# Bucketed attention and a feed-forward block on one core: the row maxima of heads 1 to 3 at new places, and four smaller moves around them

## The chip, the cores and the metric

The program runs on one core of a Trainium2 chip. The metric is the device time of one execution in microseconds (us). The core has five engines that each work through a queue of their own in order: TensorE (PE, matmuls), VectorE (DVE), ScalarE (ACT), GpSimd (POOL) and SyncE (SP), which here issues the transfers (DMAs). An instruction at the head of a queue that waits for another engine holds up everything behind it on its own engine.

## The reference

```python
q_bits = (einsum('bhsd,dk->bhsk', q, proj) > 0)      # 6 bits a row; k_bits likewise
mask   = q_bucket[..., :, None] == k_bucket[..., None, :]
scores = where(mask, q @ k.T / sqrt(64), -1e9)
attn   = exp(scores - scores.max(-1)); attn = attn / (attn.sum(-1) + 1e-9)
x      = attn @ v                                    # batch 4, 8 heads, 768 rows, width 64
h      = x_as_rows(3072, 512) @ w_in                 # 512 -> 2048
g      = where(h >= 1, h, where(h <= -1, 0, (h + 1)**2 / 4))
out    = g @ w_out                                   # 2048 -> 512
```

All of it is float32. The kernel keeps the accuracy by splitting each operand into a rounded high part and the rest, a low part, and multiplying the parts separately.

## The kernel before, in words

The 32 heads are taken in 16 pairs. A head has 12 **units**, 384 in all, numbered g from 0; head hd has the units from 12·hd. Six units cover one half of the 768 query rows, one for each block of 128 keys. The loop at the end of `attention` (L614) writes the instructions in this order for each unit:

1. `s_unit(g)`: two score matmuls (L372, L373) into one of four PSUM tiles `s`, and two exponentials on ACT (L381, L386).
2. A reduction that the unit before left over.
3. `lo_unit(g-1)`: the low part of the exponentials of the unit before, on DVE, or on POOL for the units with g mod 6 of 0 or 3.
4. `pv_unit(g-4)`: three matmuls with V (L405, L407, L409); the last of six is followed by a copy on ACT (L415) and the transfers of the result.
5. The **tasks** of the unit: whatever `at(g, ...)` put there, in the order in which the calls were made.

**Row maxima.** The mask works through extra rows of the operands: rows 0 to 7 hold the bits of both sides' buckets, and one row of the query side holds a clamped maximum of the masked scores, so that it is subtracted within the matmul. A head's maxima need six pairs of matmuls (`max_mm`, L311) into a PSUM tile `smax`, of which there is one, and six reductions on DVE (`max_red`, L315). The table `early` says where each pair goes, counted in **slots**: slot 5·g+k is in unit g, before the V matmuls (k=2), between them (k=3, 4) or behind them (k=5). For k of 2 to 4 the reduction is written at once, so on DVE it stands behind `lo_unit(g-1)`. For k=5 it is left over to the next unit, where it is written ahead of `lo_unit(g)`; the tasks of unit g stand in front of it.

**From the maxima to the query row.** Head 0 and head 1: `row_clamp` on DVE, three small matmuls on PE and a copy on ACT (`row_half`, L267) into row 32 of tile `T2[0]`. Head 2: `half_clamp` on DVE, `half_put` (a transposition on PE, a copy on ACT, two DMAs) for each half. From head 3 on: `max_clamp` on POOL (L343, L345), `max_tr` (transposition on PE, L350), `max_put` (copy on ACT, L355; two DMAs, L357 and L358). The first DMA writes row 7 of `T2`, which the second score matmul (L373) of the head reads.

**Preparing a pair.** `load_raw` brings q and k of a pair into the one tile `raw`; four times `cast_h` and `low_h` on POOL make high and low parts (L153 and L39 `t<-raw,t`), for head 0 and 1 of the pair and for the first and second half (n = 0 to 3); four `move` DMAs (L164) copy parts to other rows. `bits_mm` (four matmuls, L211), `bits_cmp` (DVE, L222), `bits_scale` (L272 or L274) and `bits_put` (four DMAs) make the bits. `load_v`, `cast_v` (ACT, L290) and `split_v` (POOL) prepare V. Pair p lives in tile p mod 3, so pair 3 takes over the tiles of pair 0, and row 32 of `T2[0]` must be cleared before that (L570).

After the attention, from about 460 us on, come the feed-forward matmuls (L829, L966, L1061). The change touches only the tasks and slots of the first 36 units, which the profile shows between 12 and 64 us.

Of the kernel before, what the change touches and what calls it, by code (L numbers as in the profile page):

```python
# [11 lines left out]
F32 = mybir.dt.float32  # L12
# [13 lines left out]
NJ = S // P  # L26
# [84 lines left out]
NU = 2 * NJ  # L111
SHIFT = 4


def attention(ctx, tc, wst, T1, T2, qk, v, pj, cv, x_d, s_d, e_d, tasks, shared):
    nc = tc.nc
# [340 lines left out]
    def at(g, fn, *a):  # L457
        tasks[g].append((fn, a))
# [79 lines left out]
    for n, g in enumerate((1, 4, 5, 6)):  # L538
        at(g, quarter, n)
    at(6, lambda: nc.gpsimd.memset(T2[1][0:64, 0].bitcast(F32), 0.0))  # L540
    at(7, row_clamp, 1, 0, NJ // 2)
    for n in (0, 1):
        at(8, move, 1, n)
    at(8, bits_mm, 1, 0, 1)
    at(9, bits_cmp, 1, 0)
    at(9, ones_row, 1, nc.vector)
    at(9, row_half, 1, 0)
    at(9, row_flags, 0)
    at(10, bits_mm, 1, 1, 0)
    at(10, split_v, 0, nc.gpsimd, 1)  # L550
# [16 lines left out]
    at(19, half_put, 2, 0, 1)  # L567
    at(23, half_clamp, 2, 1)
    at(25, half_put, 2, 1, 0)
    at(2 * NU + 1, lambda: nc.gpsimd.memset(T2[0][32:33, 0].bitcast(F32), 0.0))  # L570
    for hd in range(NH):
        pr, h = hd // 2, hd % 2
        g = hd * NU
        if 0 < hd < NH - 2:
            gc, gt = ((30, 33), (41, 43))[hd - 1] if hd < 3 else (g + NU + SHIFT - 1, g + NU + SHIFT + 1)
            at(gc, max_clamp, hd + 2, nc.gpsimd)
            at(gt, max_tr, hd + 2)
            at(gt, max_put, hd + 2)
        if h == 0 and pr + 2 < NPAIR:
            g0 = g + (13, 2)[pr] if pr < 2 else g  # L580
            for n in range(4):
                at(g0 + n, cast_h, pr + 2, nc.gpsimd, n % 2, n // 2)
                at(g0 + n, low_h, pr + 2, nc.gpsimd, n % 2, n // 2)
            at(g0 + 3, move, pr + 2, 0)
            at(g0 + 3, move, pr + 2, 1)
            at(g0 + 6, move, pr + 2, 2)
            if pr + 3 < NPAIR:
                at(g0 + 7, load_raw, pr + 3)
            bits_at = ((20, 1), (23, 0)) if pr == 0 else ((8 if pr == 1 else 7, 1), (11, 0))
            for hf, (n, bank) in enumerate(bits_at):  # L590
                at(g + n, bits_mm, pr + 2, hf, bank)
                at(g + n + 1, bits_cmp, pr + 2, hf)
            at(g + n + 1, move, pr + 2, 3)
            at(g + n + (2 if pr else 1), bits_scale, pr + 2, nc.gpsimd if pr else nc.scalar)
            at(g + (18 if pr else 25), bits_put, pr + 2)
        if h == 0 and pr + 1 < NPAIR:
            gv = g + LAG + (2 if pr else 16)
            at(gv, cast_v, pr + 1, nc.scalar)
            at(gv + 1, split_v, pr + 1, nc.gpsimd, 0)
            at(gv + 3, split_v, pr + 1, nc.gpsimd, 1)  # L600
            if pr + 2 < NPAIR:
                at(gv + (6 if pr else 4), load_v, pr + 2)
# [1 line left out]
    NG = NH * NU  # L604
    red = None
    early = {}
    for hd, gs in ((0, (0, 2)), (1, (4, 5, 6, 8, 11, 12)), (2, (15, 16, 17, 19, 20, 22)), (3, (21, 23, 24, 26, 27, 29))):
        early.update({5 * n + 5: (hd, NJ - len(gs) + i) for i, n in enumerate(gs)})
    for i in range(2 * NJ):
        n = 5 * 31 + 35 * i // 4  # L610
        early[n + (n % 5 == 1)] = 4 + i // NJ, i % NJ
# [494 lines left out]
def lsh_attn_ffn(ctx: ExitStack, tc: tile.TileContext, qk, v, pj, cv, w_in, w_out, out):  # L1106
# [101 lines left out]
    for i in (2, 3):  # L1208
        at(NH * NU + 2 * i - 10, late[i + NFT - NW1][0])
    attention(actx, tc, wst, T1, T2, qk, v, pj, cv, x_d, s_d, e_d, tasks, attn)  # L1210
    actx.close()

# [78 lines left out]
```

## Time and profile before

| | |
|---|---|
| median of 3 runs | 979.32 us (979.09 to 982.97) |
| the profiled execution | 979.4 us, of which the span is 977.6 us |
| PE busy | 961.9 us |
| DVE, ACT, POOL busy | 788.3, 680.2, 354.8 us |
| granted PE clock | 1.00 |

A row of the timeline gives the start and the duration in us, the engine, the line of the kernel, the operation, what it writes and reads, shapes, a count, and in brackets the idle time of the engine before it with what ended it. Matmuls overlap: one of 384 columns is shown with some 0.34 us, and the next starts 0.17 to 0.18 us later. SPq rows are issues of DMAs, not the transfers themselves.

### The profile page before, as it was taken

The page shows a single profiled execution, that of the slowest core. Times are in us where ns is not written, and L with a number is a line of the kernel's source. Part 1 is how long each engine was busy: PE and PEld are TensorE (multiplying, and loading weights), DVE is VectorE, ACT ScalarE, POOL GpSimd, SP SyncE. Part 2 cuts the span into 40 slices and gives each one's busy share as a digit, 9 for nine tenths or more (in the row PEclk, how much of TensorE's full clock was granted, in tenths as well). Part 3 has the DMA queues.
Part 4 walks back from the last instruction along what each step waited for, and adds up shares of the span by engine and source line. Part 5 has one row for each costly group of instructions (what it writes and reads, how often), then busy time and mean ns, then how long its engine had stood idle before and what let it go on. Part 6 is the DMA issues. An engine that isn't in the chain of part 4 may idle for free.

```text
span 977.6 us, 15547 instructions
## 1 busy us (share of the span) xinstructions
PE 961.9 (98%) x5050; PEld 890.3 (91%) x5050; DVE 788.3 (81%) x1355; ACT 680.2 (70%) x1481; POOL 354.8 (36%) x422
## 2 busy tenths in 40 slices
PE   8999999999999999999999999999999999999998
PEld 7889999999999999999999998888988888888896
DVE  8779999999999999897898788787776777655554
ACT  7888998989989998987755565455564545544444
POOL 8768887777788877566000000000000000000000
PEclk9999999999999999999999999999999999999999
DMA  5775566677666666635494479976459554454431
GB/s 161 191 183 157 153 170 177 175 191 197 179 167 166 157 175 176 153 114 134 128 335 162 139 227 300 295 241 201 119 160 236 146 183 118 148 154 119 119 87 65
DMA packets 95113, 167.56 MB, mean 171 GB/s; under 512 B 13956, under 2 KB 51960, under 8 KB 95032
## 3 DMA queue, kind: packets, MB, share of 16 engines
q1 hardware_dynamic: 94808, 166.56, 60.7%
q8 instruction: 40, 0.66, 0.3%
q14 instruction: 41, 0.34, 0.1%
q10 hardware_dynamic: 224, 0.00, 0.0%
HBM read 106.13 MB, written 33.87 MB: 143 GB/s over the span
## 4 chain that ended last, share of the span: by engine, by line
PE 86%; DVE 5%; POOL 5%; ACT 1%; issue 1%; DMA 1%; DVEq 0%; POOLq 0%; ACTq 0%
PE y L829 27%; PE h L1061 18%; PE h L966 7%; PE smax L311 6%; PE s L373 5%; PE s L372 5%; PE o L405 5%; PE o L407 5%; PE o L409 5%; POOL t L39 3%; PE o L211 2%; DVE nm L315 2%; DVE pl L39 1%; POOL pl L39 1%; POOL t L153 1%
## 5 line engine op out<-in xcount | busy, mean ns | idle before, releaser
L381 ACT ACTIVATE ph<-s 128x384 fp32r<-128x384 f32 x380 | 188.6, 496 | 41.2 <-PE s L373 36.1
L315 DVE TENSOR_REDUCE nm<-smax 128x1 f32<-128x768 f32 x189 | 179.3, 949 | 22.2 <-PE smax L311 21.0
L39 POOL TENSOR_TENSOR pl<-pf,ph 128x384 fp32r<-128x384 f32 x128 | 134.1, 1052 | 78.8 <-ACT pf L386 78.8
L794 DVE SCALAR_TENSOR_TENSOR t<-t 128x384 f32<-128x384 f32 x128 | 71.2, 557 | 101.0 <-ACT z L789 100.8
L39 DVE TENSOR_TENSOR pl<-s,ph 128x384 fp32r<-128x384 f32 x256 | 135.4, 545 | 10.9 <-ACT s L386 9.0
L372 PE MATMUL s<-t 128*128 128x384 f32 x384 | 132.2, 344 | 0.0
L373 PE MATMUL s<-t 128*128 128x384 f32 x384 | 129.6, 337 | 1.7 <-DMA t<-te 1.7
L409 PE MATMUL o<-pl,va 128*128 128x386 f32 x384 | 130.4, 340 | 0.4 <-DVE pl L39 0.4
L407 PE MATMUL o<-ph,vb 128*128 128x386 f32 x384 | 130.0, 339 | 0.0
L405 PE MATMUL o<-ph,va 128*128 128x386 f32 x384 | 129.9, 338 | 0.0
L386 ACT ACTIVATE s<-s 128x384 f32<-128x384 f32 x252 | 125.5, 498 | 0.0
L829 PE MATMUL y<-t,ghi 128*128 128x512 f32 x384 | 124.7, 395 | 0.0
L311 PE MATMUL smax<-t 128*128 128x384 f32 x378 | 100.1, 346 | 4.5 <-DVE nm L315 4.4
L788 ACT ACTIVATE t<-h,mh 128x384 f32<-128x384 f32 x56 | 32.5, 581 | 82.2 <-PE h L966 43.5
L799 ACT CAST ghi<-z 128x384 fp32r<-128x384 f32 x129 | 65.1, 505 | 30.6 <-DVE z L795 26.9
L789 ACT ACTIVATE z<-t,m 128x384 f32<-128x384 f32 x128 | 79.0, 617 | 4.2
L829 PEld LDWEIGHTS y<-t,ghi 128*128 128x128 f32 x384 | 71.3, 188 | 11.1 <-ACT ghi L799 0.3
L1061 PE MATMUL h<-wbig,t 128*128 128x384 f32 x399 | 81.4, 336 | 0.0
L311 PEld LDWEIGHTS smax<-t 128*128 128x128 f32 x378 | 66.6, 188 | 14.5 <-DVE nm L315 13.7
L1061 PEld LDWEIGHTS h<-wbig,t 128*128 128x128 f32 x399 | 71.6, 188 | 5.2
L788 ACT ACTIVATE t<-wsq,mh 128x384 f32<-128x384 f32 x48 | 29.6, 617 | 66.7 <-DVE wsq L1074 40.4
L829 PE MATMUL y<-t,glo 128*128 128x512 f32 x192 | 76.0, 396 | 0.0
(190 smaller groups left out, 2142.9 us busy)
## 6 DMA issues: line engine op xcount, KB each, us to landing
t<-wc SPq DMA_DIRECT2D x92, 256.0 KB
t<-t SPq DMA_DIRECT2D x60, 384.0 KB
wraw<-wc SPq DMA_DIRECT2D x76, 256.0 KB
raw<-in_qk_dram SPq DMA_DIRECT2D x14, 768.0 KB
wraw<-in_w_in_dram SPq DMA_DIRECT2D x16, 512.0 KB
wraw<-in_w_out_dram SPq DMA_DIRECT2D x16, 512.0 KB
t<-ed SPq DMA_DIRECT2D x36, 192.0 KB
xd<-xs SPq DMA_DIRECT2D x32, 192.5 KB
```

Source lines behind the costliest of these rows:

```text
L39: eng.tensor_tensor(out=out, in0=a, in1=b, op=ALU.subtract)
L311: nc.tensor.matmul(out=smax[hd][:, hf, 0:HS], lhsT=t2[:, 0, h, i * P:(i + 1) * P], rhs=t2[:, 1, h, hf * HS:(hf + 1) * HS], start=True, sto ...
L315: nc.vector.tensor_reduce(out=nmp(hd)[:, i:i + 1], in_=smax[hd][:, :, 0:HS], axis=AX.XY, op=ALU.max, negate=True)
L372: nc.tensor.matmul(out=ps[:, 0:HS], lhsT=t1[:, 1, h, ks], rhs=t1[:, 0, h, sl], start=True, stop=False)
L373: nc.tensor.matmul(out=ps[:, 0:HS], lhsT=t2[:, 1, h, ks], rhs=t2[:, 0, h, sl], start=False, stop=True)
L381: nc.scalar.activation(out=ph[:, 0:HS], in_=ps[:, 0:HS], func=AF.Exp, scale=SCALE)
L386: nc.scalar.activation(out=pf, in_=ps[:, 0:HS], func=AF.Exp, scale=SCALE)
L405: nc.tensor.matmul(out=o, lhsT=wa, rhs=ph, start=(jj == 0), stop=False)
L407: nc.tensor.matmul(out=o, lhsT=wb, rhs=ph, start=False, stop=False)
L409: nc.tensor.matmul(out=o, lhsT=wa, rhs=pl, start=False, stop=(jj == NJ - 1))
L829: nc.tensor.matmul(out=ys[c][m], lhsT=g_[:, m * P:(m + 1) * P], rhs=w, start=(first and k == 0), stop=(last and k == 2))
L1061: nc.tensor.matmul(out=ps, lhsT=w[:, cs], rhs=x, start=(n == 0 and s not in (2, 3, 6)), stop=(n == 5), skip_group_check=True)
```

## The change

- **Slots.** Heads 1, 2 and 3 had their maxima at k=5 of units 4, 5, 6, 8, 11, 12; 15, 16, 17, 19, 20, 22; and 21, 23, 24, 26, 27, 29. Now they stand at slots 25, 32, 40, 47, 57, 65; 72 to 109; and 117 to 150, some 7.4 slots apart, at k of 2, 4 and 5. Heads 0, 4 and later keep theirs.
- **Head 1.** The first `row_clamp` and `row_half` stand one unit later (8 and 10).
- **Pair 3** (the fourth pair). Of its four cast-and-low steps, which stood in units 26 to 29, the first two stay and the others go to 31 and 32. Its moves 0 and 1 go from unit 29 to 32, move 2 from 32 to 35, and the load of the next `raw` from 33 to 36.
- **Head 3.** `max_clamp` stays in unit 30; `max_tr` and `max_put` go from 33 to 31.
- **Row 32** is cleared by two memsets of one head each, in units 20 and 25, in place of one for both in unit 25.

```diff
-    at(7, row_clamp, 1, 0, NJ // 2)
+    at(8, row_clamp, 1, 0, NJ // 2)
...
-    at(9, row_half, 1, 0)
+    at(10, row_half, 1, 0)
...
-    at(2 * NU + 1, lambda: nc.gpsimd.memset(T2[0][32:33, 0].bitcast(F32), 0.0))
+    for h, g in enumerate((20, 2 * NU + 1)):
+        at(g, lambda h=h: nc.gpsimd.memset(T2[0][32:33, 0, h].bitcast(F32), 0.0))
...
-            gc, gt = ((30, 33), (41, 43))[hd - 1] if hd < 3 else (g + NU + SHIFT - 1, g + NU + SHIFT + 1)
+            gc, gt = ((30, 31), (41, 43))[hd - 1] if hd < 3 else (g + NU + SHIFT - 1, g + NU + SHIFT + 1)
...
-            g0 = g + (13, 2)[pr] if pr < 2 else g
+            g0 = g + (13, 5)[pr] if pr < 2 else g
             for n in range(4):
-                at(g0 + n, cast_h, pr + 2, nc.gpsimd, n % 2, n // 2)
-                at(g0 + n, low_h, pr + 2, nc.gpsimd, n % 2, n // 2)
+                gq = g0 + n - (3 if pr == 1 and n < 2 else 0)
+                at(gq, cast_h, pr + 2, nc.gpsimd, n % 2, n // 2)
+                at(gq, low_h, pr + 2, nc.gpsimd, n % 2, n // 2)
...
-    for hd, gs in ((0, (0, 2)), (1, (4, 5, 6, 8, 11, 12)), (2, (15, 16, 17, 19, 20, 22)), (3, (21, 23, 24, 26, 27, 29))):
-        early.update({5 * n + 5: (hd, NJ - len(gs) + i) for i, n in enumerate(gs)})
+    for hd, gs in ((0, (5, 15)), (1, (25, 32, 40, 47, 57, 65)), (2, (72, 79, 87, 94, 102, 109)),
+                   (3, (117, 124, 130, 137, 144, 150))):
+        early.update({n: (hd, NJ - len(gs) + i) for i, n in enumerate(gs)})
```

## The prediction

> **What bounds the kernel now.** I read the page first, then the waits of PE, then the timelines of all engines between 12 and 64 us, where the changed units run.
>
> ```profile
> span 977.6 us, 15547 instructions
> PE 961.9 (98%) x5050; PEld 890.3 (91%) x5050; DVE 788.3 (81%) x1355; ACT 680.2 (70%) x1481; POOL 354.8 (36%) x422
> ```
>
> PE is idle for 977.6 − 961.9 = 15.7 us of the whole span, so no change of order alone can be worth more. The waits of PE between 16 and 62 us, where all the moved maxima lie, and a row from the whole run:
>
> ```profile
> PE smax L311 <- DVE nm L315: 2.0, 8, 0.5
> PE o L261 <- DVE nrow L252: 0.4, 1, 0.4
> ...
> PE s L373 <- DMA t<-te: 1.7, 1, 1.7
> ```
>
> So there are two prizes: 2.0 us over eight waits of maxima for the one `smax` tile, and 1.7 us at one score matmul. Where that one comes from, on PE, on POOL and in the issues of SP:
>
> ```profile
> 54.77 0.62 PE L311 MATMUL smax<-t 128*128 128x384 f32 x2 [0.17 <-DVE nm L315]
> ...
> 58.90 0.27 PE L350 MATMUL s<-ident,nm 128*12 128x128 f32 x1
> ...
> 61.82 0.33 PE L372 MATMUL s<-t 128*128 128x384 f32 x1
> 63.85 0.44 PE L373 MATMUL s<-t 128*128 128x384 f32 x1 [1.70 <-DMA t<-te]
> ```
>
> ```profile
> 50.37 0.50 POOL L153 CAST t<-raw 128x384 fp32r<-128x384 f32 x1 [0.29 <-DMA raw<-in_qk_dram]
> ...
> 53.46 1.01 POOL L39 TENSOR_TENSOR pl<-pf,ph 128x384 fp32r<-128x384 f32 x1
> 54.42 0.50 POOL L153 CAST t<-raw 128x384 fp32r<-128x384 f32 x1
> 55.00 1.02 POOL L39 TENSOR_TENSOR t<-raw,t 128x384 fp32r<-128x384 f32 x1
> ...
> 57.53 0.23 POOL L343 TENSOR_SCALAR nm<-nm 128x6 f32<-128x6 f32 x1
> 57.84 0.23 POOL L345 TENSOR_SCALAR nm<-nm 128x6 f32<-128x6 f32 x1
> ```
>
> ```profile
> 56.49 2.42 SPq L164 DMA_DIRECT2D t<-t  x3
> 60.12 0.76 SPq L357 DMA_DIRECT2D t<-te  x1
> ```
>
> Head 3 begins with unit 36 at 61.82 and needs its row 7. The clamp came at 57.53, behind four casts, the transposition at 58.90, and the DMA was issued at 60.12, behind three moves of 384 KB issued from 56.49 on. It released PE at 63.85, 1.85 us later than the next matmul would have begun (61.82 + 0.18).
>
> **The change, part by part.**
>
> *The transposition two units sooner.* In the changed order head 3's DMA is issued ahead of the moves (units 31 and 32), and two casts stand behind the clamp instead of in front. If the clamp is in time, the 1.85 us go. The clamp can start when POOL has done two casts and the low part of unit 27, at 54.42, and when the last of head 3's reductions has ended. That end is the crux.
>
> *The spacing.* How fast can maxima follow one another through one `smax`?
>
> ```profile
> 33.92 0.62 PE L311 MATMUL smax<-t 128*128 128x384 f32 x2 [0.24 <-DVE nm L315]
> ...
> 35.59 0.62 PE L311 MATMUL smax<-t 128*128 128x384 f32 x2 [0.16 <-DVE nm L315]
> ```
>
> One per 1.67 us, if DVE is free. A spacing of 7.4 slots is 7.4 × 0.175 + 0.35 = 1.65 us of PE's work: level with that, with no slack. What matters then is where the reduction stands on DVE. At k=2 to 4 it is behind the low part of the unit before, which waits for ACT; at k=5 it was ahead of the next one. So I walk through the stretch where ACT is late. These rows of ACT, DVE and PE fix it:
>
> ```profile
> 41.88 0.83 ACT L290 CAST va<-vraw 128x768 fp32r<-128x768 f32 x1 [0.58 <-DMA vraw<-in_v_dram]
> ...
> 44.24 0.53 ACT L386 ACTIVATE s<-s 128x384 f32<-128x384 f32 x1
> ...
> 47.65 1.03 ACT L272 ACTIVATE bits<-neg,cvt 32x768 fp32r<-32x768 f32 x1
> ...
> 50.31 0.46 ACT L381 ACTIVATE ph<-s 128x384 fp32r<-128x384 f32 x1
> ```
>
> ```profile
> 42.13 0.96 DVE L315 TENSOR_REDUCE nm<-smax 128x1 f32<-128x768 f32 x1
> 43.80 0.96 DVE L315 TENSOR_REDUCE nm<-smax 128x1 f32<-128x768 f32 x1 [0.71 <-PE smax L311]
> 44.87 0.56 DVE L39 TENSOR_TENSOR pl<-s,ph 128x384 fp32r<-128x384 f32 x1
> 45.34 0.42 DVE L326 TENSOR_SCALAR nmh<-nm 128x3 f32<-128x3 f32 x1
> ...
> 45.75 0.94 DVE L315 TENSOR_REDUCE nm<-smax 128x1 f32<-128x768 f32 x1
> 46.61 0.54 DVE L39 TENSOR_TENSOR pl<-s,ph 128x384 fp32r<-128x384 f32 x1
> 47.08 0.54 DVE L222 TENSOR_TENSOR neg<-o,neg 32x384 f32<-32x384 f32 x1
> ...
> 53.76 0.96 DVE L315 TENSOR_REDUCE nm<-smax 128x1 f32<-128x768 f32 x1 [0.22 <-PE smax L311]
> ```
>
> ACT waited for V of pair 1 until 41.88. That load was issued behind the bits of pair 1 and two moves. Their start hangs on the comparison of unit 11, and in the new order one more reduction (slot 57) stands in front of that. What PE wins in units 5 to 10, some 0.6 us, is lost there, so I leave 41.88 where it is. Then unit 22's exponential ends at 44.24 + 0.53 = 44.77 as before. From there, by the new order on DVE:
>
> - low part of unit 22 at 44.8; behind it the reduction of slot 117, at 44.8 + 0.47 = 45.27, ending at 46.2. Before, head 3's first reduction had run at 42.13, inside ACT's delay.
> - slot 124 on PE at 46.3. Its reduction starts behind `half_clamp` and the low part of unit 23 (46.1 + 0.5 + 0.47), at 47.1, and takes a step of 0.87.
> - the comparison of pair 2's bits, which now stands behind that reduction: 48.0 to 48.5, against 47.08 to 47.62.
> - so ACT's bits at 48.55 instead of 47.65: 0.9 us later. ACT took from 47.65 to the row at 50.31, the first of unit 27, to finish unit 26; by that, 2.7 us, unit 26 is finished at 51.2 to 51.3, and its low part runs at 51.3.
> - the reduction of slot 137 stands behind this low part: 51.3 + 0.47 = 51.8. Slots 144 and 150 then go at the rate of the single tile, 1.67 us each: the last reduction of head 3 starts at 55.1 and ends at 56.1, against 53.76 + 0.96 = 54.72.
> - slot 155, head 4's first, waits for that and starts at 56.1, against 54.77: PE is 1.35 us **later** here than before.
>
> From there to unit 36 PE does the same work as before, 61.82 − 54.77 = 7.05 us, so unit 36 begins at 63.2 and its second matmul at 63.35. Head 3's DMA no longer stops it: clamp from 56.1 to 56.7, transposition about 57.4 (56.1 + 0.35 + a unit of 0.88), issue at some 58.5, which by the 63.85 − 60.12 = 3.7 us of the old one, moves in front of it and all, lands at 62.2.
>
> The sum: −1.85 for the wait and +1.35 for the later last reduction, −0.5 us in all.
>
> *The smaller parts.* These rows price them, the last two of SP.
>
> ```profile
> 25.25 0.47 ACT L267 CAST t<-smax 1x384 fp32r<-1x384 f32 x1
> ...
> 42.79 1.01 POOL L39 TENSOR_TENSOR vb<-vraw,va 128x384 fp32r<-128x384 f32 x1 [3.69 <-ACT va L290]
> ...
> 48.70 1.38 POOL L570 MEMSET t<- 1x1536 f32 x1
> ```
>
> ```profile
> 43.62 0.59 SPq L148 DMA_DIRECT2D raw<-in_qk_dram  x1
> ...
> 62.40 0.38 SPq L148 DMA_DIRECT2D raw<-in_qk_dram  x1
> ```
>
> Head 1's first half of the query row is copied a unit later, some 26.3 instead of 25.72 with unit 12 at about 27: hidden by one unit's matmuls, and at most the 0.47 of the copy if PE gets there early. The memset of 1.38 becomes two of about 0.69 (half the elements; between 0.2 for launch alone, as a clamp row shows, and 1.38). The first falls into POOL's idle 3.69 us before 42.79. The second saves nothing, because the casts behind it wait for `raw` at 50.37. So 0, from both sides. The three moves and the next `raw` are only issued later: nothing but head 3's two DMAs stands in between on SP, and pair 4's first cast, below, runs at 76.36, 14 us after the old issue (62.40), against 6.75 for the earlier load of that size (issued at 43.62, used at 50.37). 0 here too; at worst the three units of delay, some 3.9 us at 1.3 a unit (54.77 to 61.82 is five and a half), which that margin covers.
>
> **The rivals.**
>
> *A, the whole prize.* If DVE is not held up as I walk it, for instance because V lands sooner, the last reduction stays at 54.72 or before. Then the clamp is bound by POOL alone, 54.42 + 0.5 = 54.9, and PE passes the transposition at about 55.0, where unit 32 began at 56.09 before: 1.05 us sooner, and 1.85 more at unit 36, together 2.9. Time 979.4 − 2.9 = 976.5. For it speaks that PE's work there leaves room. Against it, the single tile at 1.67 per maximum.
>
> ```profile
> 56.09 0.33 PE L372 MATMUL s<-t 128*128 128x384 f32 x1
> ```
>
> *B, slower: POOL becomes the bound at unit 35.* The two casts behind the clamp are needed by the second `bits_mm` of pair 3 there. In my walk POOL goes from the clamp's end, 56.7, through four subtractions at 0.96 (unit 30's low part, one split of V, two low halves of the pair; 53.46 to 54.42 is such a step) and two casts at 0.58 (54.42 to 55.00): 56.7 + 4 × 0.96 + 2 × 0.58 = 61.7. PE comes to it at 63.2 − 0.7 = 62.5, 0.8 us of slack. Later in the run POOL's rows are longer:
>
> ```profile
> L39 POOL TENSOR_TENSOR t<-raw,t 128x384 fp32r<-128x384 f32 x12 | 12.1, 1016 | 0.8
> ...
> 76.36 0.96 POOL L153 CAST t<-raw 128x384 fp32r<-128x384 f32 x1
> ...
> 79.91 1.35 POOL L39 TENSOR_TENSOR t<-raw,t 128x384 fp32r<-128x384 f32 x1
> ```
>
> At 1.35 and 0.96 the same queue takes 4 × 0.34 + 2 × 0.46 = 2.3 more, 1.5 over the slack, and the sum is −0.5 + 1.5 = +1.0: 980.4. It decides from 0.8 us of stretching on; over 1.3 us the kernel is slower. Against it: the twelve subtractions between 12 and 70 us took 1016 ns on average. [...]
>
> *C, it does not do what it says.* The maxima wait as much as before, in other places, and head 3's row is late again, since the clamp follows a last reduction about 2.8 us later than before (57.5): no gain, 979.4.
>
> **How the numbers follow.** My sum is against the profiled execution, 979.4, which stands 0.1 over the median of 979.32. The forecast is 979.4 − 0.5 = 978.9, with a range of its own of 978.0 to 979.8. Chances: forecast 0.5, A 0.27, B 0.13, C 0.1. The range that takes in A and B is 976.2 to 980.8. A measurement of this kernel can tell about 0.5%, 4.9 us, from no change. All my cases lie within that. The bound for more is the sum of all waits of PE in this stretch, 2.0 + 1.7 + 0.4 = 4.1 us with 0.1 to restart after each of ten, 5.1. So faster 0.03, same 0.95, slower 0.02, the rest for causes that I don't see.
>
> **What would show it.** Right: no wait of L373 for `te`; the bits of pair 2 on ACT at 48 to 49; a wait of over 1 us of a maximum for DVE near 51 to 53; PE's waits of L311 for L315 in this stretch well over 2.0 us; slot 155 past 55.5. A is right if the bits stay at 47.65 or earlier and unit 36 begins before 61.5. B shows as a wait of L211 for POOL near 62. The sum is wrong if V lands at another time than 41.9, since the whole walk hangs on it.

## The result, and the profile after

The changed kernel takes 984.33 us in the median of 15 executions (981.82 to 989.01), the kernel before 980.22 (978.86 to 983.4). The ratio is 1.0039, 95% interval 1.0029 to 1.0050: slower by 0.4%, where 0.05% less was forecast. The profiled execution is 7.0 us longer in its span. Page and PE clock by slices:

```profile
span 984.6 us, 15537 instructions
PE 965.2 (98%) x5050; PEld 894.5 (91%) x5050; DVE 787.5 (80%) x1355; ACT 680.0 (69%) x1481; POOL 355.2 (36%) x423
...
PEclk9899999999999999999999999999999999999999
```

The second slice, 25 to 49 us, has a clock below 9 tenths. By stretches (length, then busy time with counts of PE, weight loads, DVE, ACT, POOL; then the granted clock):

```profile
24.00:36.00 12.00, 8.58 (x44) 7.66 (x44) 7.15 (x14) 7.02 (x17) 9.90 (x14) 0.85 0.49 132
36.00:48.00 12.00, 10.71 (x52) 9.97 (x51) 7.56 (x12) 8.61 (x22) 5.82 (x8) 0.86 0.71 176
...
72.00:100.00 28.00, 26.26 (x140) 25.44 (x139) 22.98 (x35) 22.76 (x55) 19.03 (x22) 0.94 0.65 169
```

At a clock of either 1.0 or 0.5, the only two values in the trace's record of it, a mean of 0.85 is 3.6 us at half of it (12 × 0.15 / 0.5), 0.86 is 3.4, 0.94 in 28 us is 3.4: 10.4 us at half clock. (The record itself has 0.5 from 32.51 to 39.34 us and from 83.71 to 87.12, 10.24 us.) The kernel before had 1.00 in all such stretches:

```profile
24.00:36.00 12.00, 11.31 (x63) 9.53 (x62) 8.59 (x14) 10.79 (x25) 11.00 (x15) 1.00 0.53 135
36.00:48.00 12.00, 11.58 (x64) 10.33 (x62) 10.34 (x19) 8.96 (x21) 6.34 (x8) 1.00 0.88 236
```

The waits of PE in the changed kernel between 12 and 100 us (total, times, longest):

```profile
PE smax L311 <- DMA t<-bits: 2.7, 1, 2.7
PE s L373 <- DMA t<-te: 1.7, 1, 1.7
PE o L405 <- DVE neg L222: 1.7, 2, 1.0
PE smax L311 <- DVE nm L315: 1.6, 3, 1.1
PE o L334 <- ACT s L386: 0.5, 1, 0.5
```

The total of waits for reductions has fallen to 1.6 us, from 2.8 in the kernel before over the same stretch, and two waits for transfers head the list. PE's timeline at both places, and at unit 36:

```profile
30.07 0.34 PE L372 MATMUL s<-t 128*128 128x384 f32 x1
30.25 0.33 PE L373 MATMUL s<-t 128*128 128x384 f32 x1
33.27 0.98 PE L311 MATMUL smax<-t 128*128 128x384 f32 x2 [2.69 <-DMA t<-bits]
34.04 0.53 PE L405 MATMUL o<-ph,va 128*128 128x386 f32 x1
34.36 0.53 PE L407 MATMUL o<-ph,vb 128*128 128x386 f32 x1
...
59.79 0.34 PE L372 MATMUL s<-t 128*128 128x384 f32 x1
...
68.06 0.34 PE L372 MATMUL s<-t 128*128 128x384 f32 x1
68.23 0.33 PE L373 MATMUL s<-t 128*128 128x384 f32 x1
...
81.15 0.34 PE L372 MATMUL s<-t 128*128 128x384 f32 x1
83.23 0.44 PE L373 MATMUL s<-t 128*128 128x384 f32 x1 [1.74 <-DMA t<-te]
...
84.30 0.53 PE L407 MATMUL o<-ph,vb 128*128 128x386 f32 x1
```

Unit 14 begins at 30.07, as before (30.08). Slot 72, head 2's first maximum, then waits 2.69 us for pair 1's bits, and the matmuls behind it take 0.53 instead of 0.34 and start 0.32 apart instead of 0.175. Unit 36 goes through without the old stop. At 81.15 unit 48, head 4's first, stops for its row in the way unit 36 used to, and slow matmuls follow again. Head 2's first maximum in the kernel before, at slot 80, for comparison:

```profile
32.22 0.59 PE L311 MATMUL smax<-t 128*128 128x384 f32 x2
```

The first score matmul of a unit shows where each kernel stands. The table gives how many us later than in the kernel before it starts, in the profiled executions. The ratio compares the medians with executions of the kernel before from the same measurement; medians of different rows can come from different measurements. "full" counts the timed executions with a mean granted clock of 0.999 or more.

| kernel | unit 12 | 16 | 30 | 37 | 60 | median, us | ratio to before, 95% | full |
|---|---|---|---|---|---|---|---|---|
| changed | +0.54 | +5.03 | +6.24 | +4.27 | +7.06 | 984.33 | 1.0029 to 1.0050 | 3 of 15 |
| e6 slot 72 alone | −0.11 | +1.32 | +0.57 | +0.58 | +0.57 | 980.43 | 1.0002 to 1.0020 | 9 of 11 |
| e1 slots alone | +4.00 | +7.09 | +8.27 | +6.55 | +6.55 | 982.73 | 1.0023 to 1.0042 | 3 of 12 |
| e2 pair 3 alone | +0.15 | −0.07 | −0.31 | −2.25 | −1.30 | 979.40 | 0.9984 to 1.0010 | 7 of 12 |
| e3 slots 80, 83 | +0.14 | +0.66 | +2.95 | +0.99 | +3.01 | 983.83 | 1.0022 to 1.0051 | 2 of 5 |
| e5 fillers | +0.23 | +2.72 | +3.16 | +1.20 | +2.26 | 982.96 | 1.0014 to 1.0039 | 8 of 12 |
| e7 e3, bits 44 | +0.73 | +1.23 | +3.49 | +1.54 | +2.02 | 981.88 | 0.9999 to 1.0019 | 9 of 11 |
| e8 e2, bits 44 | +0.24 | +0.06 | −0.17 | −2.09 | −1.97 | 978.58 | 0.9964 to 0.9989 | 11 of 12 |
| e9 e3, head 3 old | +0.34 | +0.84 | +1.65 | −0.30 | +0.89 | 982.23 | 1.0001 to 1.0025 | 3 of 11 |
| e10 e9, slots 50, 60 | +1.61 | +1.26 | +2.08 | +0.14 | +1.06 | 981.19 | 0.9994 to 1.0024 | 6 of 12 |
| e11 e1, other clamp | +0.28 | +2.77 | +3.19 | +2.86 | +2.85 | 982.25 | 1.0004 to 1.0024 | 4 of 12 |
| e12 e8, other clamp | −0.37 | −0.37 | −0.59 | −2.19 | −1.97 | 978.08 | 0.9960 to 0.9980 | 11 of 11 |
| e13 e10, other clamp | +0.74 | +0.38 | +1.20 | −0.75 | +0.41 | 981.43 | 0.9991 to 1.0013 | 5 of 12 |

From unit 60 to unit 380 most of them keep their distance to within half a microsecond; e5, e7 and e9 lose another 0.9 to 1.3. Of the kernel before, 20 of 29 executions beside e1 were full, with a median of 979.26; the other nine had 981.48. Of the changed kernel the three full ones had 982.13 and the twelve others 985.47. So, as far as two measurements compare, about 2.9 us of the loss are there at full clock; the rest of the median's 4.1 goes with the clock.

### The profile page after: what moved, and what is told of

It reads as the page before. It is cut to its first block, busy times and chain, and to the rows that moved or that the text cites. A ratio compares the mean times of both kernels' runs of the same rounds, so it can differ in the third digit from the quotient of the medians.

```text
span 984.6 us, 15537 instructions
## 1 busy us (share of the span) xinstructions
PE 965.2 (98%) x5050; PEld 894.5 (91%) x5050; DVE 787.5 (80%) x1355; ACT 680.0 (69%) x1481; POOL 355.2 (36%) x423
## 4 chain that ended last, share of the span: by engine, by line
PE 87%; POOL 5%; DVE 4%; ACT 1%; issue 1%; DMA 1%; SPq 0%; DVEq 0%; POOLq 0%
PE y L832 27%; PE h L1064 18%; PE h L969 7%; PE smax L311 6%; PE s L373 5%; PE s L372 5%; PE o L405 5%; PE o L407 5%; PE o L409 5%; POOL t L39 3%; PE o L211 2%; DVE nm L315 1%; POOL pl L39 1%; DVE pl L39 1%; POOL t L153 1%
## 5 line engine op out<-in xcount | busy, mean ns | idle before, releaser
L315 DVE TENSOR_REDUCE nm<-smax 128x1 f32<-128x768 f32 x189 | 179.3, 949 | 27.7 <-PE smax L311 26.7
L311 PE MATMUL smax<-t 128*128 128x384 f32 x378 | 100.4, 347 | 6.2 <-DVE nm L315 3.1
L311 PEld LDWEIGHTS smax<-t 128*128 128x128 f32 x378 | 67.5, 190 | 14.5 <-DVE nm L315 10.8
L832 PE MATMUL y<-woh,glo 128*128 128x512 f32 x192 | 75.7, 394 | 0.2
```

Source lines behind the costliest of these rows:

```text
L311: nc.tensor.matmul(out=smax[hd][:, hf, 0:HS], lhsT=t2[:, 0, h, i * P:(i + 1) * P], rhs=t2[:, 1, h, hf * HS:(hf + 1) * HS], start=True, sto ...
L315: nc.vector.tensor_reduce(out=nmp(hd)[:, i:i + 1], in_=smax[hd][:, :, 0:HS], axis=AX.XY, op=ALU.max, negate=True)
L832: nc.tensor.matmul(out=ys[c][m], lhsT=g_[:, m * P:(m + 1) * P], rhs=w, start=(first and k == 0), stop=(last and k == 2))
```

## The experiments

The theory formed after the result, W, is that PE stops for transfers that the change calls for too early (pair 1's bits) or issues too late (head 4's row), and that a stop lowers the clock. Its rival, D, is the prediction's own: the order of the reductions on DVE. Each variant's expectation stands as it was written before the variant ran.

**One slot alone (e6).**

```diff
-(2, (15, 16, 17, 19, 20, 22))     # slots 80, 85, 90, 100, 105, 115
+(2, (13.4, 16, 17, 19, 20, 22))   # slots 72, 85, 90, 100, 105, 115, by int(round(5 * n)) + 5
```

> The kernel before with one pair of matmuls moved: head 2's first maximum from slot 80 (behind the V matmuls of unit 15) to slot 72 (before those of unit 14); everything else as before. Theory W (a maximum that comes too early for its data): pair 1's bit rows, written by four DMAs issued in unit 12, have not landed; PE stops for 1.5 to 2.7 us near 31 to 33 us in a wait of L311 for a DMA t<-bits, and in most executions the granted clock falls to 0.5 for some microseconds afterwards; 981 to 985 us against about 980 of the kernel before. Theory D (the order of the reductions on DVE, as the prediction walked it): one reduction's place alone costs at most 0.5 us, 979.5 to 980.5, full clock throughout.

Measured: a wait of 1.55 us, as W expected, and 980.43 us, as D did.

```profile
31.91 0.59 PE L311 MATMUL smax<-t 128*128 128x384 f32 x2 [1.55 <-DMA t<-bits]
```

The wait comes with the slot alone. The mean clock stayed at 0.999 or more in 9 of 11 executions, against W, and of the 1.9 us lost at unit 15 only 0.6 are left at unit 28. So the wait at this place was for the most part made up behind it, in a profiled execution with a mean clock of 0.999.

**The slots alone, and pair 3 alone (e1, e2).**

e1 is the kernel before with the new slots of heads 1 to 3 and `row_clamp` and `row_half` in units 8 and 10. e2 is the changed kernel with the old slots and these two in units 7 and 9.

> The kernel before with the new slots of heads 1 to 3 and head 1's row one unit later; pair 3's casts, moves and load, head 3's transposition and the memset as before. Theory W: the wait for pair 1's bits of 2 to 2.7 us and a stretch at clock 0.5 as in the changed kernel; the wait of head 3's second score matmul for te at unit 36 stays or is longer; no such wait at unit 48; 983 to 987 us. Theory D: the new slots alone cost the 1.35 us of the prediction's walk, 981 to 982, full clock.

> The changed kernel with the old slots and head 1's row at its old units: pair 3's casts, moves and load of raw later, head 3's transposition two units sooner, a memset per head. Theory W: the wait at unit 36 (1.7 us) is gone; head 4's row for unit 48 is issued behind the DMAs that were moved and PE waits for it there, 1 to 2 us, with a stretch at clock 0.5 in some executions; 978 to 982 us. Theory D: only the gain of 1.85 us is left, 978 to 978.5, no wait at unit 48.

Measured: e1 982.73, just outside the ranges of both theories, with the wait for bits (2.48), two stretches at half clock, and, unforeseen by both, 2.45 us of PE behind a DVE that stood still (below). Against W's expectation e1 had no wait at unit 36, although its transposition was not moved: PE came there 8.3 us later than in the kernel before, and the row had landed. e2 979.40: unit 36 goes through with PE on time, unit 37 is 2.25 us sooner, 1.96 of it won between units 36 and 37 (predicted: 1.85), and a wait of 1.07 us comes at unit 48.

```profile
76.04 0.44 PE L373 MATMUL s<-t 128*128 128x384 f32 x1 [1.07 <-DMA t<-te]
```

So most of the loss is in the slots, and the moved DMAs of pair 3 cost something that was priced at nothing.

**Bits before they are needed (e3), and fillers (e5).**

```diff
 e3: -(2, (72, 79, 87, 94, 102, 109))
     +(2, (80, 83, 87, 94, 102, 109))
 e5, in max_mm, ahead of head 2's first pair:
     +for _ in range(24):
     +    keep_busy(smax[hd][:, 0])
```

> The changed kernel with head 2's first two maxima at slots 80 and 83 in place of 72 and 79. Theory W: no wait of a maximum for DMA t<-bits over 0.5 us, clock 1.00 between 24 and 48 us, units 15 to 28 some 4 us sooner than in the changed kernel; the wait at unit 48 may stay; 979 to 982 us. Theory D: the rest of the order on DVE is as in the changed kernel, so the time stays within 1.5 us of it, 983 to 985.

> The changed kernel with 24 idle matmuls of 256 columns (some 2.6 us) written into the maxima's tile just ahead of slot 72, so that PE has something to do while pair 1's bits are on their way; the real matmuls write over them. Theory W with the clock: slot 72 starts no more than 0.5 us later than in the changed kernel, the clock stays at 1.00 there, units 15 to 20 lose what the wait takes (about 3 to 4.5 us against the kernel before) and no more; the median falls by 0.5 to 2 us against the changed kernel's 984.3. If the half clock has nothing to do with PE standing still, it comes as before, and the fillers make it slower: 985 and up.

Measured: e3 had no half clock in its profile and unit 16 at +0.66 instead of +5.03, but a wait of 1.03 us for the bits was left, and the median of its five executions, 983.83, is in D's range and not in W's. Both theories have a part: +2.95 at unit 30 is there at full clock, against the +1.35 of the prediction. In e5 slot 72 came 0.3 us sooner than in the changed kernel, and at full clock:

```profile
30.11 3.03 PE L429 MATMUL smax<-idle 128*128 128x256 f32 x24
32.98 0.56 PE L314 MATMUL smax<-t 128*128 128x384 f32 x2
```

```profile
24.00:36.00 12.00, 11.39 (x76) 10.96 (x76) 7.45 (x13) 8.07 (x20) 10.59 (x14) 1.00 0.49 129
36.00:48.00 12.00, 10.70 (x60) 9.79 (x59) 8.72 (x17) 9.02 (x23) 7.48 (x9) 1.00 0.81 208
```

Nearly three microseconds of useless matmuls (30.11 to 32.98) didn't make the kernel slower. The median is 982.96 against 984.33, but the intervals of the two ratios overlap, and among full executions e5 is not faster (982.69 against 982.13). What differs more clearly is the clock: 8 of 12 executions were full instead of 3 of 15. At unit 18 e5 is 1.4 us behind the kernel before, the changed kernel 4.5. The profile of e5 alone doesn't tie the half clock to PE standing still, because e11, described below, has the changed kernel's wait of 2.69 us for the bits without fillers, and its profile shows no half clock:

```profile
PE smax L313 <- DMA t<-bits: 2.7, 1, 2.7
...
PEclk9999999999999999999999999999999999999999
```

e11 stands at +1.46 at unit 18 and at +3.19 at unit 30, where e3 with a wait of 1.03 has +2.95 and the changed kernel +6.24. So at full clock the wait is nearly made up, and some 3 us of the changed kernel's lateness at unit 30 are the half clock. How the two stops lie on the steps of the clock's record is in the last section.

**The bits of pair 3 behind head 4's row (e7, e8).**

```diff
-            at(g + (18 if pr else 25), bits_put, pr + 2)
+            at(g + (20 if pr == 1 else 18 if pr else 25), bits_put, pr + 2)
```

> The changed kernel with head 2's first maxima at slots 80 and 83 and, besides, pair 3's four bit DMAs issued in unit 44, behind head 4's row, in place of unit 42. Theory W: the wait for te at unit 48 (1.7 to 2.1 us) is gone or under 0.5; the time falls against the kernel with slots 80 and 83 alone by that, 979 to 981.5, and what is left over the kernel before is DVE's order, about 3 us at unit 30. Theory D has no place for unit 48: no change against 983.8.

> The old slots, pair 3's and head 3's moves of the change, and pair 3's bit DMAs in unit 44 behind head 4's row. Theory W: no wait for te at unit 36 nor at unit 48, unit 60 some 2.5 us sooner than in the kernel before; 976.5 to 978.5 in the median, faster than both kernels. If the row of unit 48 is late for another reason (transfers in front of it on the rings), the wait of 1.1 us stays and the time is that of the variant without this shift, 979.4.

Measured: the wait at unit 48 went from 2.14 us in e3 to 0.6 in e7, a little over W's 0.5, and from 1.07 in e2 to 0.2 in e8. e7's 981.88 and e8's 978.58 lie just above W's ranges; e8 is faster than the kernel before, ratio 0.9977. SP's issues in the kernel before, in the changed kernel, and then in e8:

```profile
70.33 2.76 SPq L283 DMA_DIRECT2D t<-bits  x4
73.48 0.75 SPq L357 DMA_DIRECT2D t<-te  x1
```

```profile
69.93 1.69 SPq L148 DMA_DIRECT2D raw<-in_qk_dram  x1
73.02 0.47 SPq L164 DMA_DIRECT2D t<-t  x1
...
76.63 3.15 SPq L283 DMA_DIRECT2D t<-bits  x4
81.05 0.75 SPq L357 DMA_DIRECT2D t<-te  x1
```

```profile
64.25 1.72 SPq L148 DMA_DIRECT2D raw<-in_qk_dram  x1
...
71.40 0.79 SPq L357 DMA_DIRECT2D t<-te  x1
72.24 0.44 SPq L358 DMA_DIRECT2D ed<-te  x1
72.79 3.42 SPq L283 DMA_DIRECT2D t<-bits  x4
```

In the kernel before the four bit DMAs stood ahead of head 4's row too, but they were through at 73.09, before ACT had copied the row (73.22 + 0.24), and the row was issued 3.4 us ahead of unit 48 (76.88). In the changed kernel the later load and moves of pair 3 push the bit DMAs back in SP's queue: they begin 1.9 us after unit 42 (74.72) and not with it, the row, copied at 77.73, waits for them until 79.78 and another 1.2 us for a move, and is issued at 81.05, 0.1 us ahead of unit 48 (81.15).

**Head 3's places (e9).**

```diff
-(3, (117, 124, 130, 137, 144, 150))     # on e3
+(3, (110, 120, 125, 135, 140, 150))
```

> The changed kernel with slots 80 and 83 for head 2 and, besides, head 3's six maxima at their old places behind the V matmuls (110, 120, 125, 135, 140, 150). Theory D for the stretch from unit 23 on: the wait of over 1 us of a maximum for a reduction near 50 to 58 us goes, and unit 30 stands at most 1.5 us behind the kernel before instead of 2.95; 981.5 to 983 in the median. If the lateness at unit 30 comes from the transfers and not from DVE's order, unit 30 stays 2.5 to 3 us behind.

Measured: unit 30 at +1.65, a little over the 1.5 that was expected, 982.23 us. Some 1.3 of the 2.95 us are head 3's spacing; what is left is there by unit 20 (+1.9), which is in front of head 3's slots.

**The comparisons ahead of the reductions (e10, e13).**

```diff
-(1, (25, 32, 40, 47, 57, 65))           # on e9
+(1, (25, 32, 40, 50, 60, 65))
```

> The variant with slots 80 and 83 and head 3's old places, in which besides two maxima of head 1 go from slots 47 and 57 (ahead of the V matmuls of units 9 and 11, so their reductions stand ahead of pair 1's comparisons on DVE) to 50 and 60 (behind them, so the comparisons come first). If the comparisons behind a reduction are what makes pair 1's bits and V late: ACT's bits of pair 1 start at 28.0 to 28.2 instead of 28.76, with no wait for DVE's neg of 0.76; V of pair 1 is cast at 41.3 to 42.1 instead of 42.9; units 16 to 20 stand 0.3 to 1.2 us behind the kernel before instead of 0.8 to 1.9; unit 30 at most 1.0 behind instead of 1.65. If the lateness there comes from head 2's places alone, nothing of this moves.

> The variant with head 1's maxima at slots 50 and 60, slots 80 and 83 for head 2 and head 3's old places, now with the clamp by a reduction, so that DVE isn't held up there: to be read against the variant with slots 47 and 57 whose clamp took 0.28 us. If a comparison behind a reduction is what makes pair 1's bits and V late: ACT's bits of pair 1 start at 27.6 to 28.2 (28.76 there) with no wait for neg, V of pair 1 is cast at 41.2 to 42.1 (42.9 there), unit 16 stands within 0.4 us of the kernel before (0.84 behind there) and unit 30 at most 1.0 behind (1.65 there). If not, these stay where they are.

Measured: e10 can't be read, since its clamp held DVE for 1.99 us. In e13 ACT no longer waits for the comparison. Its rows, and before them those of e9:

```profile
28.76 1.03 ACT L272 ACTIVATE bits<-neg,cvt 32x768 fp32r<-32x768 f32 x1 [0.76 <-DVE neg L222]
...
42.91 0.82 ACT L290 CAST va<-vraw 128x768 fp32r<-128x768 f32 x1
```

```profile
28.32 1.01 ACT L272 ACTIVATE bits<-neg,cvt 32x768 fp32r<-32x768 f32 x1
...
42.46 0.82 ACT L290 CAST va<-vraw 128x768 fp32r<-128x768 f32 x1
```

V follows the bits by 14.1 us in both, as expected of the chain, but both are only 0.45 us sooner and miss their ranges (28.2 and 42.1 at the latest): PE now waits 1.2 us for a reduction in `row_half` at unit 10, ahead of the matmuls for the second comparison. Unit 16 met its expectation (+0.38), unit 30 missed it (+1.20). Which of head 2's places makes the rest was not separated.

**A clamp by a reduction (e11, e12).**

```diff
-nc.vector.tensor_scalar(out=nrow[hd][:, a:b, 32], in0=nms[hd][:, a:b], scalar1=CLAMP, op0=min)
+both = nms[hd].rearrange("p (t j) -> p j t", t=2)       # second half holds CLAMP
+nc.vector.tensor_reduce(out=nrow[hd][:, a:b, 32], in_=both[:, a:b, :], axis=X, op=min)
```

> The kernel with the new slots of heads 1 to 3 alone, in which the clamp of head 1's and head 0's maxima on DVE (L252, a tensor-scalar minimum over 128x3) is made by a reduction instead: the minimum of a maximum and a constant beside it, also 128x3 results. [...]

> The variant with the old slots, pair 3's and head 3's moves and the bits of pair 3 in unit 44, with the same clamp by a reduction. [...]

The question was whether the long clamp of e1, 4.12 us, goes with the form of the instruction. Measured: all four clamps took 0.15 to 0.17 us in both kernels. In e11 PE's longest wait for neg is 1.0 us (2.45 in e1), and unit 12 stands at +0.28 (+4.00 in e1). DVE in the changed kernel, where three instructions end together at 24.54, as POOL's memset does (23.14 + 1.37 = 24.51), and then in e11:

```profile
22.54 2.00 DVE L252 TENSOR_SCALAR nrow<-nm 128x3 fp32r<-128x3 f32 x1
23.14 1.40 DVE L39 TENSOR_TENSOR pl<-s,ph 128x384 fp32r<-128x384 f32 x1
23.60 0.94 DVE L315 TENSOR_REDUCE nm<-smax 128x1 f32<-128x768 f32 x1
```

```profile
23.14 1.37 POOL L540 MEMSET t<- 64x1536 f32 x1
```

```profile
22.38 0.15 DVE L253 TENSOR_REDUCE nrow<-nm 128x3 fp32r<-128x6 f32 x1
22.45 0.55 DVE L39 TENSOR_TENSOR pl<-s,ph 128x384 fp32r<-128x384 f32 x1
```

The clamp in unit 8 took 2.00, 4.12, 0.28, 0.29, 1.98, 0.28 and 1.99 us in the profiles of the changed kernel, e1, e3, e5, e7, e9 and e10; the reduction took 0.15 to 0.17 in all twelve cases of e11 to e13. So POOL being busy is not enough for a long clamp; what decides between 0.28 and 2 us or more was not separated. e12 has the lowest median, 978.08, ratio 0.9970, and each of its executions was full; its interval overlaps that of e8.

## Why the prediction was wrong

- **"So I leave 41.88 where it is": the first step that failed.** The walk set out from a unit 22 that was on time. At full clock (e3) V of pair 1 was cast at 42.73 and unit 22 stood at +1.52; in the changed kernel's profile it was 46.02 and +4.81. One reason is the comparison behind slot 57's reduction: ACT waited 0.76 us for it in e3, e5, e7, e9 and e11, and with the comparisons first (e13) 0.45 us of that was won. The lateness arises in units 14 to 20, where head 2's new slots are (from −0.40 to +1.70 in e3); how the rest of it divides was not taken apart.
- **The later last reduction, +1.35: right.** Between units 22 and 30 all six profiles with the new slots of head 3 (the changed kernel, e1, e3, e5, e7, e11) lose 1.40 to 1.43 us. It came on top of the lateness at unit 22: ACT's bits of pair 2 were at 50.15 in e3, where 48.55 was predicted. The slots of head 3 are in fact 6.6 apart, closer than the 7.4 that was reckoned with, but the walk itself used the tile's 1.67 us there.
- **"The transposition two units sooner", −1.85: right.** Between units 36 and 37 the changed kernel won 1.97 us, e2 1.96 (−0.29 to −2.25). The sign, no wait at unit 36, was by itself no proof, since e1 shows it without the moved transposition. The proof is in e2, with PE on time, and in e11, where the old place left a wait of 1.36 us.
- **"The three moves and the next `raw` are only issued later ... 0": wrong.** The margin was reckoned for `raw` alone. What is queued behind on SP was not followed past unit 36: head 4's row released PE 1.9 us late in the changed kernel (83.23 against 81.15 + 0.18), 1.7 of it shown as a wait. From unit 48 to unit 60 e3 loses 2.02 us and e7 0.49, e2 0.95 and e8 0.12.
- **What is due at a new slot: missing.** The walk asked of each moved maximum when `smax` and DVE are free, and not whether its operands had landed. Slot 72 needs two DMAs issued in unit 12. Before, at 32.22, PE didn't wait for them, and e6 had them at 31.91, so they were just there; in the changed kernel that was a wait of 2.69 us.
- **The clock: missing.** The prediction had no rival in which a stop costs more than its length. 10.4 us at half clock are worth up to 5.2 of the 7.0 us in the profile; e5, at full clock, is at +2.26 at unit 60 instead of +7.06.
- **"Head 1's row a unit later: hidden": wrong in its price.** The copy was hidden, but the clamp in its new place took up to 4.12 us (e1), where it had taken 0.56. In the changed kernel, with a clamp of 2.00 us, that shows as 0.4 us at units 12 and 14 (+0.54 and 0.00, against +0.14 and −0.40 in e3).
- **The signs and the rivals.** A wait of over 1 us for a reduction came (1.12 us, at 57.66), but PE's waits of L311 for L315 between 16 and 62 us fell from 2.0 to 1.3 us instead of rising. B, POOL at unit 35, did not come: its subtractions stayed at 1.01 and there was no wait of L211. A, the whole prize at −2.9, is what e8 and e12 come near to (−2.0 at unit 60) once the slots stay where they were. No rival held the result.

In e3, at full clock, the prediction's sum reads so: +1.5 up to unit 22 (predicted 0), +1.4 from there to unit 30 (+1.35), −2.0 at unit 36 (−1.85), +2.0 from unit 48 to unit 60 (0), together +3.0 in place of −0.5. The full executions of the changed kernel agree, 982.13 against 979.26, though only three of them were full. The other 4 us of the changed kernel's profile go with its two stretches at half clock and the longer wait for the bits.

## What to carry to other kernels

When work moves forward in a queue, list for each of its operands when it lands, and when a DMA moves back, follow everything issued behind it to the next user. In this kernel, with PE busy for 98% of the span, a stop could cost more than its length: behind stops of 2.69 and 1.74 us the changed kernel had 10.24 us at half clock, and e11, with a stop of 2.69 us too, had none. So take the granted clock of every execution, and compare executions at full clock before reading a difference of a few microseconds. An even spacing isn't a gain in itself where the places between had been chosen around data and comparisons.

## What the runs showed of the hardware

- **The four stretches at half clock in the changed kernel and e1 came behind steps of 3.41 us in which PE had been idle for 1.74 to 2.45 us; e11's stop of 2.69 us, which lay across two steps, went without.** In the traces' records of the clock, in all fourteen profiles, changes lie whole multiples of 3.41 us apart: the changed kernel's half clock lasts 6.83 us from 32.51 and 3.41 us from 83.71, and these starts are 51.20 us or 15 steps apart. With the trace laid on these steps, PE was idle for 1.93 and 1.74 us of the step just before the two stretches, and for 2.45 and 2.00 us before the two of e1. No other step between 12 and 110 us of any profile has more than 1.82 us (e11), 1.70 (the kernel before) and 1.67 (e6), and none was followed by half clock. An edge cuts e11's stop of 2.69 us into 1.82 and 0.87, and e3's of 2.14 into 0.59 and 1.55. The traces give no sharp border, since 1.74 was followed by half clock and 1.82 was not. Why one stretch lasted two steps is not shown. Only the profiled executions have such records: e13's has no step with more than 0.94 us idle, and yet 7 of its 12 timed executions were not full, so where those lost their clock stays open.
- **A tensor-scalar instruction on DVE of three elements a partition took up to 4.12 us while POOL worked without a gap, and the instructions behind it ended with it; the same minimum as a reduction took 0.15 to 0.17.** The 4.12 us of e1, from 22.72 to 26.84, lie beside five POOL instructions in a row, the last of which ended at 26.81. The same clamp took 0.28 us in e3 (22.27 to 22.55), beside POOL's subtractions from 20.53 to 23.49, and 0.29 and 0.28 in e5 and e9.
